# Gated linear attention and an expert layer on one core: attention from the second chunk on in halves of 64 tokens, with a new instruction order

## The chip, the core and the metric

The kernel runs on one core of a Trainium2 chip. The metric is the device time of one execution in microseconds (us), taken as the median of several runs. One execution was also recorded by the hardware profiler; that record is "the trace". PE is TensorE, DVE VectorE, ACT ScalarE, POOL GpSimd, and SP is the engine that issues the DMAs. Matrix products read SBUF and write PSUM, which has eight banks of 128 partitions by 512 fp32 numbers.

## What is computed

Two things follow each other: a recurrent attention with exponential gates over 4 batches, 8 heads, 768 tokens and head width 40, and a dense layer of width 320 to 2048 to 320 on its output.

```python
for t in range(S):
    m_new = np.maximum(f_gate[:, :, t] + m, i_gate[:, :, t])
    f_stab = np.exp(f_gate[:, :, t] + m - m_new)
    i_stab = np.exp(i_gate[:, :, t] - m_new)
    C = f_stab * C + i_stab * outer(vt, kt)
    n = f_stab * n + i_stab * kt
    y[:, :, t] = sigmoid(o_gate) * (C @ qt) / max(abs(n @ qt), 1.0)
x = y.transpose(0, 2, 1, 3).reshape(B * S, H * D)
h = x @ w_in
g = h * erf(softplus(h))
out = g @ w_out
```

All inputs are fp32; the two weight matrices arrive as 64-bit numbers and are decoded on the chip into a high and a low part.

## The kernel before

**Attention.** The 768 tokens are cut into 6 chunks of 128. A step s is one chunk of one batch, so there are 24 steps; chunk c = s // 4. Within a step the recurrence is written as matrix products. `S` forms 128 by 128 scores per head (L509). The decay between two tokens stands in the tile `dm`: for the first `PEX` = 6 steps PE builds it (`pe`, L426 to L429) and ACT takes its exponential; for the other 18 steps it is read back from DRAM by a broadcasting DMA (`bq`, L446), POOL adds a column (`add`, L450), ACT takes the exponential (`ex`, L454) and POOL zeroes the upper triangle (`sel`, L459). DVE multiplies scores and decay (`w`, L525). `ph` then makes the output: queries times the state carried over from the chunk before (L543), weights times values (L547), and the step's own contribution to the next state (L552), from values scaled by `vg` (L517). The state is a tile of 104 partitions by 4 by 82; two heads share it as a block-diagonal matrix whose other blocks are zero. `sa` (L562) and `sk` (L577) carry it on. `yg` (L583 to L587), `y` (L593) and `yy` (L599) normalise and gate, `tr` (L605) transposes, and `xh` (L621) and `xl` (L639) split the result into a high and a low part.

**Dense layer.** The 12 blocks of 256 tokens go through 24 phases. A phase has four `up` pieces on PE (L840, products of high and low parts in fp32r), each copied out of PSUM by `hb` (L851 on DVE, L849 on ACT), then softplus and erf on ACT (`sp` L863, `er` L867), their product on DVE (`mu` L875), a high part on ACT (`gh` L881), a low part on DVE (`gl` L886), and four `dn` pieces on PE (L921, L922, L924; for the first two phases full fp32, L917). ACT copies the sums out (`o`, L944). Weights are loaded and decoded in the first third of the run.

**Order.** Every engine executes its own queue in order. The order is written out by hand of a planner: the list `SEQUENCE` names each piece of work, and the program issues them one after the other. `+n` stands for n filler products on PE (L253), which compute nothing that is used. From step 10 on the pieces `tr(s-2)`, `S(s)` and `ph(s-1)` are merged into one (`X`), so that they stand directly behind each other on PE. Which engine does a copy is fixed by sets such as

```python
HB_ACT = {0, 1, 4}
VG_POOL = {3, 4, 5, 6, 7}
```

Of the kernel before, what the change touches and what calls it, by code (L numbers as in the profile page):

```python
# [18 lines left out]
L = 128  # L19
# [5 lines left out]
V1 = D + 1  # L25
# [56 lines left out]
SLOTS = dict(bank=6, po0=1, po1=1, big=20, xx=4, vg=2, dq=2, bits=2, den=2, gt=1, m_c=2, x0=2, aT=2, spl=1)  # L82
BANKS = dict(pa=4, h=2, po2=1, po3=1)
EARLY = 3
FULL = 2
# [3 lines left out]
HB_ACT = {0, 1, 4}  # L89
HI_DVE = {'i00', 'i01', 'i20', 'o4', 'o6', 'o9'}  # L90
LO_DVE = {'i01', 'i10', 'i20', 'i31', 'o1', 'o4', 'o5', 'o8', 't2', 't3'}
LO_PE = {'i00', 'i01', 'o0', 'o1', 'o4', 'o9', 't0', 't1', 't2'}
GL_POOL = set()
# [3 lines left out]
PEX = 6  # L97
# [4 lines left out]
VG_POOL = {3, 4, 5, 6, 7}  # L102
SK_ACT = {1, 2}
Y_DVE = {0, 1, 5, 6, 7, 9}
# [12 lines left out]
w2.1 lpi00 ex3.1 scan1 ph2 deci10 vali11 loi00 S3 load5 yg2 vg3 sk2.0 wout3 sk2.1 tr1 hii10 deci11 tr0 +1 loadv5
+1 xh0 +1 loadv7 +1 loi10 xh1 +1 wout8 +1 hii11 +1 xl1 y2 +2 valo2 +1 xl0 +1 loi11 +1 w3.0 up0.0 w3.1 yy2 valo4
deco2 up0.1 hb0.0 deco4 hio2 valo3 sum1 ph3 hb0.1 deco3 cumw1 th5 tr2 gexp1 up0.2 sp0.0 sk3.0 loo2 wout0 yg3
wout1 rest1 up0.3 hb0.2 hio4 gload2 sk3.1 y3 xh2 loadv4 hio3 xl2 yy3 decw1 tr3 loo4 hb0.3 at1 +2 xh3 atc1 loo3  # L120
+2 sp0.1 +1 xl3 +2 up1.0 split1 er0.0 up1.1 scan2 dq4 er0.1 mu0.0 dq5 valo0 pe4.0 sum2 th4 valo8 pe4.1 mu0.1
cumw2 hb1.0 ex4.0 up1.2 deco8 rest2 ex4.1 bq6 deco0 at2 th7 S4 hio8 atc2 vg4 hb1.2 pe5.1 w4.0 valo1 pe5.0 loo8
hio0 qa4 up1.3 vali20 w4.1 loo0 ex5.0 ex5.1 hb1.1 deci20 S5 hb1.3 sp1.0 deco1 ph4 hii20 qa5 dn0.1 wout6 hio1
loi20 er1.0 loo1 bq7 sa4 dn0.0 yg4 vg5 dq7 add6 sp1.1 sk4.1 w5.1 dn0.2 w5.0 sk4.0 y4 er1.1 mu1.0 ph5 add7 dn0.3
valo6 yg5 wout9 o0.0 yy4 deco6 tr4 o0.1 load8 dn1.0 mu1.1 xh4 win31 valo9 hio6 tail1 xl4 loo6 dn1.1 win21 deco9
y5 win30 dn1.3 hio9 load7 vali31 yy5 sa5 deci31 dq6 tr5 lpo9 sk5.0 hii31 wout7 sk5.1 xh5 loi31 wout5 dn1.2
vali21 xl5 loo9 deci21 valt1 up2.0 hii21 load6 dect1 load9 o1.0 o1.1 loi21 hit3 up2.1 hb2.0 hit2 vali30 lot3
lot2 up2.2 hb2.1 valo5 deci30 sp2.0 up2.3 hb2.2 deco5 hii30 up3.0 er2.0 hb2.3 loi30 up3.1 hb3.0 hio5 mu2.0 valo7
up3.2 hb3.1 gh2.0 deco7 sp3.0 up3.3 gl2.0 hb3.2 sp2.1 dn2.1 hb3.3 hio7 loo5 sp3.1 loo7 up4.0 er2.1 dn2.0 er3.1
mu2.1 up4.1 hb4.0 mu3.1 gh2.1 loadv6 er3.0 up4.2 gl2.1 ex6 bq8 mu3.0 dn2.3 hb4.2 sel6 dn2.2 gexp2 gh3.0 decw2  # L130
vg6 ex7 gl3.0 S6 gload3 o2.0 o2.1 S7 add8 w6.1 hb4.1 w6.0 th6 dn3.0 gh3.1 qa6 qa7 ph6 gl3.1 dn3.1 scan3 bq9
loadv8 yg6 sel7 sum3 dn3.2 loadv9 sa6 cumw3 rest3 dn3.3 sk6.1 vg7 w7.0 dq8 add9 sk6.0 th8 o3.0 up4.3 w7.1 st3.0
th9 o3.1 ex9 y6 st3.1 yy6 ph7 ex8 sel9 sp4.0 sel8 S8 yg7 bq10 load10 tr6 vg8 up5.0 w8.0 load11 xh6 loadv10 hb4.3
qa8 er4.0 w8.1 up5.1 y7 vg9 yy7 hb5.0 add10 tr7 xl6 ph8 xh7 loadv11 hb5.1 xl7 sp5.0 mu4.0 up5.2 bq11 sa8 sa7
gh4.0 dq9 sk8.1 up5.3 sk7.0 sp4.1 sk7.1 dq10 gl4.0 er4.1 S9 sk8.0 add11 yg8 dn4.0 w9.1 ex10 y8 w9.0 qa9 dn4.1
mu4.1 th11 th10 at3 yy8 hb5.2 X10 gload4 gh4.1 sel10 atc3 hb5.3 gl4.1 sp5.1 tr8 vg10 bq12 dn4.3 scan4 loadv12
er5.0 w10.0 sa9 dn4.2 yg9 dq11 ex11 sk9.1 mu5.0 up6.0 sk9.0 add12 load12 w10.1 th12 up6.1 o4.0 xh8 hb6.0 st4.0
gh5.0 sel11 xl8 ex12 o4.1 up6.2 hb6.1 st4.1 er5.1 sel12 up6.3 y9 hb6.2 sp6.0 yy9 mu5.1 up7.0 hb6.3 vg11 gh5.1
up7.1 qa10 sp6.1 gl5.1 er6.0 X11 sum4 gl5.0 cumw4 gexp3 mu6.0 dn5.1 bq13 er6.1 w11.0 decw3 yg10 dn5.0 qa11 gh6.0
w11.1 y10 hb7.0 xh9 dn5.2 yy10 add13 xl9 hb7.1 up7.2 sp7.0 o5.0 sa10 st5.0 mu6.1 dq12 up7.3 hb7.2 gh6.1 sk10.0  # L140
# [892 lines left out]
```

## Time and profile before

| | |
|---|---|
| median of 3 runs (lowest to highest) | 471.83 us (471.32 to 472.54) |
| the profiled execution's own time | 472.8 us |
| its span, first to last instruction | 471.1 us |
| PE busy | 457.5 us, 97% |
| DVE busy | 335.0 us, 71% |
| ACT busy | 337.8 us, 72% |
| POOL busy | 105.1 us, 22% |
| DMA | 53.21 MB, 113 GB/s on average |

Busy time is the union of an engine's instructions. A share near 100% on one engine says that the others wait for it over the span as a whole; in which stretch that holds, and what is lost in the rest, has to be read by stage.

### The profile page before, as it was taken

The page shows a single profiled execution, that of the slowest core. Times are in us where ns is not written, and L with a number is a line of the kernel's source. Part 1 is how long each engine was busy: PE and PEld are TensorE (multiplying, and loading weights), DVE is VectorE, ACT ScalarE, POOL GpSimd, SP SyncE. Part 2 cuts the span into 40 slices and gives each one's busy share as a digit, 9 for nine tenths or more (in the row PEclk, how much of TensorE's full clock was granted, in tenths as well). Part 3 has the DMA queues.
Part 4 walks back from the last instruction along what each step waited for, and adds up shares of the span by engine and source line. Part 5 has one row for each costly group of instructions (what it writes and reads, how often), then busy time and mean ns, then how long its engine had stood idle before and what let it go on. Part 6 is the DMA issues. An engine that isn't in the chain of part 4 may idle for free.

```text
span 471.1 us, 12874 instructions
## 1 busy us (share of the span) xinstructions
PE 457.5 (97%) x5569; PEld 404.0 (86%) x5574; DVE 335.0 (71%) x565; ACT 337.8 (72%) x390; POOL 105.1 (22%) x99
## 2 busy tenths in 40 slices
PE   9899999999989999699999999999999999999997
PEld 3468877999979999689899988899988889888996
DVE  4689998767979888479669568777727775646460
ACT  3658994897597976276997579999269547778561
POOL 2213161216342124104022532131220020000000
PEclk9999999999999999899999999999999999999999
DMA  7993449412664028703023861022720000001001
GB/s 192 407 384 106 148 143 295 172 58 88 193 254 144 30 82 210 217 21 116 0 90 106 239 184 48 14 94 86 195 79 3 0 3 1 0 1 56 1 0 58
DMA packets 28877, 53.21 MB, mean 113 GB/s; under 512 B 3060, under 2 KB 17844, under 8 KB 28820
## 3 DMA queue, kind: packets, MB, share of 16 engines
q1 hardware_dynamic: 28820, 52.38, 35.6%
q8 instruction: 44, 0.72, 0.7%
q14 instruction: 13, 0.11, 0.1%
HBM read 48.27 MB, written 4.10 MB: 111 GB/s over the span
## 4 chain that ended last, share of the span: by engine, by line
PE 85%; DMA 8%; issue 2%; DVE 2%; SPq 2%; ACT 1%; DVEq 0%; ACTq 0%
PE h L840 35%; PE po L921 12%; PE po L924 11%; PE po L922 11%; PE pa L509 4%; PE po L917 4%; DMA raw<-in_w_out_dram 3%; PE pa L543 3%; PE pa L547 2%; DMA raw<-in_w_in_dram 2%; DMA qk<-in_qk_dram 2%; PE pa L605 1%; DMA kvo<-in_kvo_dram 1%; PE pa L552 1%; DVE bits L787 1%
## 5 line engine op out<-in xcount | busy, mean ns | idle before, releaser
L840 PE MATMUL h<-xx,wh 128*128 128x256 f32 (+1 forms) x768 | 177.4, 339 | 2.6 <-issue 2.0
L840 PEld LDWEIGHTS h<-xx,wh 128*128 128x128 f32 x768 | 126.8, 189 | 18.8 <-issue 2.0
L922 PE MATMUL po<-wol,gh 128*128 128x320 f32 x352 | 106.1, 310 | 3.7 <-issue 3.7
L921 PE MATMUL po<-woh,gh 128*128 128x320 f32 x352 | 107.9, 316 | 0.0
L851 DVE COPY hb<-h 128x512 f32<-128x512 f32 x84 | 57.5, 688 | 54.0 <-PE h L840 53.1
L840 PE MATMUL h<-xx,wl 128*128 128x256 f32 (+1 forms) x256 | 86.5, 338 | 0.0
L924 PE MATMUL po<-woh,gl 128*128 128x320 f32 x352 | 76.9, 311 | 0.0
L922 PEld LDWEIGHTS po<-wol,gh 128*128 128x128 f32 x352 | 66.5, 189 | 4.8 <-issue 3.9
L875 DVE TENSOR_TENSOR hb<-e,hb 128x1024 f32<-128x1024 f32 x44 | 56.5, 1290 | 16.6 <-ACT e L867 16.4
L921 PEld LDWEIGHTS po<-woh,gh 128*128 128x128 f32 x352 | 66.3, 188 | 2.1
L886 DVE TENSOR_TENSOR gl<-hb,gh 128x1024 fp32r<-128x1024 f32 x44 | 55.8, 1268 | 15.1 <-ACT gh L881 15.0
L863 ACT ACTIVATE e<-hb 128x1024 f32<-128x1024 f32 x48 | 50.3, 1058 | 22.0 <-DVE hb L851 21.7
L881 ACT ACTIVATE gh<-hb 128x1024 fp32r<-128x1024 f32 x44 | 46.2, 1050 | 19.1 <-DVE hb L875 16.6
L924 PEld LDWEIGHTS po<-woh,gl 128*128 128x128 f32 x352 | 58.3, 189 | 0.1
L840 PEld LDWEIGHTS h<-xx,wl 128*128 128x128 f32 x256 | 48.4, 189 | 5.7
L867 ACT ACTIVATE e<-e 128x1024 f32<-128x1024 f32 x48 | 50.0, 1057 | 0.4
L450 POOL TENSOR_TENSOR dm<-dm,aT 128x1024 f32<-128x1024 f32 x18 | 37.7, 2094 | 43.6 <-DVE dm L525 23.5
L867 ACT ACT_TABLE_LOAD x36 | 46.2, 1283 | 0.6
L863 ACT ACT_TABLE_LOAD x33 | 42.3, 1283 | 4.6 <-DVE hb L851 4.1
L593 POOL TENSOR_TENSOR kvo<-kvo,den 128x320 f32<-128x320 f32 x18 | 16.6, 920 | 108.3 <-DVE kvo L587 56.6
L459 POOL TENSOR_SCALAR_AFFINE_SELECT dm<-dm 128x1024 f32<-128x1024 f32 x18 | 21.9, 1220 | 67.6 <-ACT dm L454 66.5
L525 DVE TENSOR_TENSOR dm<-pa,dm 128x512 f32<-128x512 f32 x48 | 32.0, 683 | 6.2 <-PE pa L509 6.0
(116 smaller groups left out, 561.4 us busy)
## 6 DMA issues: line engine op xcount, KB each, us to landing
kvo<-in_kvo_dram SPq DMA_DIRECT2D x24, 484.0 KB
dm<-cum_dr SPq DMA_DIRECT2D x18, 512.0 KB
qk<-in_qk_dram SPq DMA_DIRECT2D x12, 512.0 KB
qk<-in_qk_dram SPq DMA_DIRECT2D x12, 416.0 KB
raw<-in_w_in_dram SPq DMA_DIRECT2D x8, 512.0 KB
out_dram<-o SPq DMA_DIRECT2D x24, 160.0 KB
raw<-in_w_out_dram SPq DMA_DIRECT2D x8, 320.0 KB
dq<-dec_dr SPq DMA_DIRECT2D x20, 128.0 KB
```

The lines of the kernel that those rows point to most:

```text
L450: nc.gpsimd.tensor_tensor(v.dm, v.dm, G.aT[:, b].unsqueeze(2).to_broadcast([128, H, L]), op=ALU.add)
L525: nc.vector.tensor_tensor(v.w[:, j], v.ps[j], v.w[:, j], op=ALU.mult)
L840: nc.tensor.matmul(V.h[i][:, n * width:(n + 1) * width], w, m, start=(q == 0), stop=(q == len(ops) - 1))
L851: nc.vector.tensor_copy(V.hb[:, i * 512:(i + 1) * 512], V.h[i])
L863: nc.scalar.activation(V.e, V.hb, AF.Softplus)
L867: nc.scalar.activation(V.e, V.e, AF.Erf)
L875: nc.vector.tensor_tensor(V.g if full else V.hb, V.e, V.hb, op=ALU.mult)
L881: nc.scalar.activation(V.gh, V.hb, AF.Copy)
L886: (nc.gpsimd if f in GL_POOL else nc.vector).tensor_tensor(V.gl, V.hb, V.gh.bitcast(F32), op=ALU.subtract)
L921: nc.tensor.matmul(po, V.gh[:, ts], woh[:, w], start=start, stop=False)
L922: nc.tensor.matmul(po, V.gh[:, ts], wol[:, w], start=False, stop=False)
L924: nc.tensor.matmul(po, V.gl[:, ts], woh[:, w], start=False, stop=stop)
```

## The change

The change has these parts.

- From the second chunk on each step works on two halves of 64 tokens. Scores are 64 by 64 per half and head. Between the halves there is a middle state (`mid`), made from the state before by `ma` and `mk` on DVE; `na` and `nk` make the state after the second half. A state is now a new tile of 104 by 4 by 41 without zero blocks.
- `S` holds the scores and the contribution to the two states; it therefore needs `vg`, which needs `sel`. `ph` holds queries times state and weights times values, written side by side into two PSUM banks; `hc` copies the first of them to SBUF, and `yg` adds the second in two more operations.
- The decay tile is half as large. `PEX` is 4, so PE builds it for 4 steps and 20 steps read it from DRAM.
- Copies and subtractions get an engine one by one through the table `ENGINES`. Among 24 phases, `hb` runs 60 times on ACT and 36 on DVE (before 12 and 84), `gh` 20 times on ACT and 24 on DVE (44 and 0), `gl` 27 times on DVE and 17 on POOL (44 and 0), `vg` 8 on DVE and 16 on POOL (15 and 5).
- `SEQUENCE` is new throughout. It has 15 filler products where there were 56. `ph` is no longer merged with the pieces beside it; `tr(s-2)` and `S(s)` still are (`A`) for most steps.

```diff
-PEX = 6
+PEX = 4
+HL = L // 2
...
+            for t in (slice(0, HL), slice(HL, L)) if c else (slice(0, L),):
+                nc.vector.tensor_tensor_scan(out=x[:, C, t], data0=x[:, Y, t], data1=zero.to_broadcast([128, t.stop - t.start]),
+                                             initial=0.0, op0=ALU.add, op1=ALU.add)
...
             def bq():
-                v.dm = big("dm").rearrange("p (h l) -> p h l", l=L)
+                t = big("dm")[:, 0:H * HL]
+                v.dm = t.rearrange("p (h l) -> p h l", l=HL)
                 v.w = ofj(v.dm)
-                nc.sync.dma_start(v.dm, cum_dr[c, b:b + 1].to_broadcast([128, H, L]))
+                for g, r in enumerate(half_rows):
+                    nc.sync.dma_start(v.dm[r], cum_dr[c, b, g:g + 1].to_broadcast([HL, H, HL]))
...
             def sl():
-                nc.gpsimd.affine_select(out=v.dm, in_=v.dm, pattern=[[0, H], [1, L]], compare_op=ALU.is_ge,
-                                        fill=0.0, base=0, channel_multiplier=-1)
+                for r in half_rows:
+                    nc.gpsimd.affine_select(out=v.dm[r], in_=v.dm[r], pattern=[[0, H], [1, HL]], compare_op=ALU.is_ge,
+                                            fill=0.0, base=0, channel_multiplier=-1)
...
+            @make(f'S{s}', 'PE', 0.95 if not last else 0.8, 128 if not last else 96, after=[load, loadv, *ex, *vg], new=psb, use=[qkb, kvb, vgb], mode=1,
+                  target=due - 2 * lead, order=[step[s - 1].ph_] if s < 5 else [step[s - 2].ph_])
+            def Sp():
+                banks()
+                for p in range(NPR):
+                    for g, r in enumerate(half_rows):
+                        for j in range(2):
+                            js = slice(64 * j, 64 * j + D)
+                            nc.tensor.matmul(v.ps[j][r, p], v.k[js, p, r], v.q[js, p, r], start=True, stop=True)
+                kf = v.kn.rearrange("p h d -> p (h d)")
+                for p in range(NPR):
+                    for j in range(2):
+                        for g, r in enumerate(half_rows[0:1] if last else half_rows):
+                            m, at = 64 if j == 0 else D, (2 * p + j) * D
+                            nc.tensor.matmul(v.pk[g][64 * j:64 * j + m, p], kf[r, at:at + m], v.vg[r, 2 * p + j],
+                                             start=True, stop=True)
...
+            mid = carried('m', 'mid', lambda: prev.st, 0, prev.next, new=[midb], use=[prev.nextb])
+            if not last:
+                v.next = [carried('n', 'st', lambda: v.mid, 1, [mid], new=[v.nextb], use=[midb])]
...
+            for p in range(NPR):
+                for g, r in enumerate(half_rows):
+                    for j in range(2):
+                        js = slice(64 * j, 64 * j + D)
+                        nc.tensor.matmul(v.ph[j][r, 0, p], v.q[js, p, r], (v.mid if g else prev.st)[js, p], start=True, stop=True)
+            for h in range(H):
+                for i in range(2):
+                    for g, r in enumerate(half_rows):
+                        o = slice(32 * i, 32 * i + 32)
+                        nc.tensor.matmul(v.ph[h % 2][HL * g + 32 * i:HL * g + 32 * i + 32, 1, h // 2], v.w[r, h % 2, h // 2, o], v.v1[r, h],
+                                         start=True, stop=True)
...
     for s in range(CLUSTER, steps + 1):
-        plan.merge(f'X{s}', [*([step[s - 2].tr] if s > CLUSTER else []), *([step[s].S] if s < steps else []), step[s - 1].ph_])
+        m = [*([step[s - 2].tr] if s > CLUSTER else []), *([step[s].S] if s < steps else [])]
+        if len(m) > 1:
+            plan.merge(f'A{s}', m)
```

How the order changes is shown at two places. The first is PE's queue at one attention step. Before, in the last chunk (where no state is made), transposition, scores and output stand behind each other between two `dn` pieces:

```order
L605 MATMUL pa<-ident,kvo 128x128 x3
L509 MATMUL pa<-qk 128x128 x8
L543 MATMUL pa<-state_71,qk 32x82 x4
L547 MATMUL pa<-kvo,dm 32x41 x8
L543 MATMUL pa<-state_71,qk 32x82 x4
L547 MATMUL pa<-kvo,dm 32x41 x8
L543 MATMUL pa<-state_71,qk 32x82 x4
L547 MATMUL pa<-kvo,dm 32x41 x8
L543 MATMUL pa<-state_71,qk 32x82 x4
L547 MATMUL pa<-kvo,dm 32x41 x8
L921 MATMUL po_4129<-woh,gh 128x320
```

After, at a step of the third chunk, the transposition and the scores with the state products (L544, L550) stand between an `up` piece and a `dn` piece:

```order
L880 MATMUL h<-xx,wh 128x256 x2
L659 MATMUL pa<-ident,kvo 128x128 x3
L544 MATMUL pa<-qk 64x64 x16
L550 MATMUL pa<-vg,kvo 64x41 x2
L550 MATMUL pa<-vg,kvo 40x41 x2
L550 MATMUL pa<-vg,kvo 64x41 x2
L550 MATMUL pa<-vg,kvo 40x41 x2
L550 MATMUL pa<-vg,kvo 64x41 x2
L550 MATMUL pa<-vg,kvo 40x41 x2
L550 MATMUL pa<-vg,kvo 64x41 x2
L550 MATMUL pa<-vg,kvo 40x41 x2
L958 MATMUL po_2634<-woh,gh 128x320
```

and the output of a step stands further on, alone between dense products:

```order
L880 MATMUL h<-xx,wh 128x256 x2
L607 MATMUL pa<-st,qk 64x41 x16
L612 MATMUL pa<-kvo,dm 32x41 x32
```

So each step of the later chunks now interrupts the dense products twice instead of once. Counted over PE's whole queue, neighbouring products with different tilings of the array (rows by columns that one product occupies) meet 124 times after and 99 times before.

The second place is POOL's queue in the middle of the run. Before, it holds additions, selections and the scaling of outputs only:

```order
L450 TENSOR_TENSOR dm<-dm,aT 128x1024
L593 TENSOR_TENSOR kvo<-kvo,den 128x320
L599 COPY kvo<-kvo 128x64
L459 AFFINE_SELECT dm<-dm 128x1024
L450 TENSOR_TENSOR dm<-dm,aT 128x1024
L459 AFFINE_SELECT dm<-dm 128x1024
```

After, low parts of the dense layer (L923) stand in the same queue, ahead of `add`, `sel` and `vg` (L487, L497, L513):

```order
L513 TENSOR_TENSOR vg<-kvo,dm 128x328
L923 TENSOR_TENSOR gl<-hb,gh 128x1024
L487 TENSOR_TENSOR dm<-dm,aT 128x512
L497 AFFINE_SELECT dm<-dm 64x512 x2
L647 TENSOR_TENSOR kvo<-kvo,den 128x320
L513 TENSOR_TENSOR vg<-kvo,dm 128x328
```

What moved is a part of DVE's work for the dense layer onto POOL, in front of the chain that ends in `vg`, for which `S` on PE now waits.

## Rows read from the trace of the kernel before

**Rows 1.** The page: busy times, and the chain that ended last by engine.
```profile
PE 457.5 (97%) x5569; PEld 404.0 (86%) x5574; DVE 335.0 (71%) x565; ACT 337.8 (72%) x390; POOL 105.1 (22%) x99
PE 85%; DMA 8%; issue 2%; DVE 2%; SPq 2%; ACT 1%; DVEq 0%; ACTq 0%
```
**Rows 2.** Windows of 20 us: stretch, its length, busy (count) per engine, clock, DMA.
```profile
40.00:60.00 20.00, 19.31 (x167) 15.92 (x158) 19.28 (x41) 18.54 (x30) 5.89 (x7) 1.00 0.49 153
180.00:200.00 20.00, 16.34 (x218) 15.02 (x217) 12.48 (x22) 7.75 (x11) 7.39 (x7) 0.91 0.88 231
400.00:420.00 20.00, 20.00 (x112) 17.95 (x111) 12.18 (x14) 15.29 (x14) 0.00 (x0) 1.00 0.00 0
```
**Rows 3.** Waits of PE: line, for what, total us, times, longest.
```profile
PE po L922 <- issue: 3.7, 1, 3.7
PE h L840 <- issue: 2.0, 1, 2.0
```
**Rows 4.** Timeline of PE, one merged step: start, us, engine, line, operation.
```profile
323.53 0.49 PE L605 MATMUL pa<-ident,kvo 128*128 128x128 f32 x3
323.95 1.16 PE L509 MATMUL pa<-qk 40*128 40x128 f32 x16
325.04 0.35 PE L543 MATMUL pa<-state,qk 104*32 104x82 f32 x8
325.20 0.33 PE L547 MATMUL pa<-kvo,dm 128*32 128x41 f32 x16
325.36 0.33 PE L543 MATMUL pa<-state,qk 104*32 104x82 f32 x8
...
326.24 0.48 PE L552 MATMUL pa<-vg,kvo 128*32 128x41 f32 x32
326.65 0.42 PE L921 MATMUL po<-woh,gh 128*128 128x320 f32 x1
326.91 0.31 PE L922 MATMUL po<-wol,gh 128*128 128x320 f32 x1
327.06 0.31 PE L921 MATMUL po<-woh,gh 128*128 128x320 f32 x1
```
**Rows 5.** Timeline of PE, a transposition alone between dense products.
```profile
391.82 0.49 PE L605 MATMUL pa<-ident,kvo 128*128 128x128 f32 x3
392.07 0.39 PE L921 MATMUL po<-woh,gh 128*128 128x320 f32 x1
```
**Rows 6.** Timeline of PE, the decay of one early step, then fillers.
```profile
7.98 0.38 PE L426 MATMUL pa<-mask 128*128 128x512 bf16 x1
9.69 2.35 PE L253 MATMUL po<-warm 128*128 128x512 bf16 x10
```
**Rows 7.** Groups by line: out<-in, shape, count | busy us, mean ns | idle before.
```profile
L547 PEld LDWEIGHTS pa<-kvo,dm 128*32 128x32 f32 x1536 | 25.3, 110 | 3.1 <-issue 1.8 <-ACT dm L438 0.8 <-DVE dm L525 0.4
L509 PEld LDWEIGHTS pa<-qk 40*128 40x128 f32 x384 | 23.2, 187 | 3.6 <-issue 1.9 <-PE pa L605 0.5 <-PE po L924 0.2
```
**Rows 8.** Groups by line on DVE, ACT and POOL.
```profile
L851 DVE COPY hb<-h 128x512 f32<-128x512 f32 x84 | 57.5, 688 | 54.0 <-PE h L840 53.1
L849 ACT ACTIVATE hb<-h 128x512 f32<-128x512 f32 x12 | 7.1, 589 | 1.0 <-PE h L840 1.0
L881 ACT ACTIVATE gh<-hb 128x1024 fp32r<-128x1024 f32 x44 | 46.2, 1050 | 19.1 <-DVE hb L875 16.6 <-PE h L840 2.6
L886 DVE TENSOR_TENSOR gl<-hb,gh 128x1024 fp32r<-128x1024 f32 x44 | 55.8, 1268 | 15.1 <-ACT gh L881 15.0
L450 POOL TENSOR_TENSOR dm<-dm,aT 128x1024 f32<-128x1024 f32 x18 | 37.7, 2094 | 43.6 <-DVE dm L525 23.5 <-DMA dm<-cum_dr 14.1 <-DVE kvo L593 3.3
L517 POOL TENSOR_TENSOR vg<-kvo,dm 128x328 f32<-128x328 f32 x5 | 5.4, 1085 | 18.1 <-DVE m_c L311 9.4 <-DMA dq<-dec_dr 8.5
```
**Rows 9.** Timeline of DVE: one low part.
```profile
185.47 2.96 DVE L886 TENSOR_TENSOR gl<-hb,gh 128x1024 fp32r<-128x1024 f32 x1 [1.12 <-ACT gh L881]
```
**Rows 10.** Windows of 2 us around PE's longest stop; columns as in rows 2.
```profile
190.00:192.00 2.00, 0.00 (x0) 0.00 (x0) 0.36 (x1) 0.38 (x1) 0.53 (x2) 1.00 0.83 325
194.00:196.00 2.00, 2.00 (x10) 2.00 (x9) 0.47 (x1) 0.00 (x0) 0.00 (x0) 0.50 0.96 234
```

More of the change, by code (lines that the diff above doesn't have):

```diff
@@ L117 @@
[L117 to L121, printed above, removed]
@@ L404, in attention @@
         if c > 0:
[L405 removed]
+            @make(f'dq{s}', 'SP', 1.16, after=[G.dec], kb=350.0, new=[dqb])
             def dqp():
@@ L511, in attention, with values, vgp @@
-        v.S = Sp
         vg, w = [], []
-        if not last:
-            @make(f'vg{s}', *(('POOL', 0.8) if s in VG_POOL else ('DVE', 0.52)), after=[*sel, loadv], new=[vgb], use=[dmb, kvb], lock=True)
-            def vgp():
+        def values():
+            @make(f'vg{s}', 'DVE', on=dict(DVE=0.52, POOL=0.8), after=[*sel, loadv], new=[vgb], use=[dmb, kvb], lock=True)
+            def vgp(e):
                 v.vg = t = new(sb, [128, H, V1], F32, "vg")
-                (nc.gpsimd if s in VG_POOL else nc.vector).tensor_tensor(
-                    t, v.v1, v.dm[:, :, L - 1:L].to_broadcast([128, H, V1]), op=ALU.mult)
+                engines[e].tensor_tensor(
+                    t, v.v1, v.dm[:, :, Q - 1:Q].to_broadcast([128, H, V1]), op=ALU.mult)
@@ L522, in attention @@
+        v.S = Sp
         for j in range(2):
-            @make(f'w{s}', 'DVE', 0.69, after=[Sp, sel[j]], use=[psb[j], dmb], order=vg)
+            @make(f'w{s}', 'DVE', 0.4 if c else 0.69, after=[Sp, sel[j]], use=[psb[j], dmb], order=vg)
             def wp(j=j):
@@ L526, in attention @@
             w.append(wp)
-        qa = None
+        qa = mid = None
+        v.next = []
         if c > 0:
@@ L580, in yg, with sk, hcopy @@
-        @make(f'yg{s}', 'DVE', 0.97, after=[ph, th], new=[denb], use=[phb, kvb])
+        if c == 0:
+            @make(f'sk{s}', 'DVE', on=dict(DVE=0.3, ACT=0.38), after=[ph], new=[v.nextb], use=phb, target=due + 10)
+            def sk(e):
+                v.st = new(sb, [128, NPR, V1], F32, "st")
+                copy_on(e, v.st[0:QR], v.pk[0:QR])
+            v.next = [sk]
+        hj, hc = lambda j: v.v1.rearrange("p (n j) d -> p j n d", j=2)[:, j], []
+        for j in range(2) if c else ():
+            @make(f'hc{s}', 'ACT', on=dict(ACT=0.3, DVE=0.28), after=[ph], use=[phb[j], kvb])
+            def hcopy(e, j=j):
+                copy_on(e, hj(j), v.ph[j][:, 0])
+            hc.append(hcopy)
@@ L647, in decode @@
     def decode(name, raw, rawb, ready, hi, lo):
-        engine = 'DVE' if name in LO_DVE else 'POOL'
         v = SimpleNamespace()
@@ L772, in weights_out @@
         name, vb = f'o{u}', Buf('bits')
-        engine = 'DVE' if name in LO_DVE else 'POOL'
         n, o = divmod(u, 2)
```

438 lines of the change are left out of this document (216 added, 222 removed).

## The prediction

> **What bounds the kernel now.** I read the page first: PE is busy 97% of the span, DVE 71%, ACT 72%, POOL 22%, and the chain that ended last lies on PE for 85% of the span [rows 1]. A share over the span says little about stages, so the windows come next. After the start-up PE is full; 400 to 420 us shows it, with 20.00 of 20 us, while DVE needs 12.18 and ACT 15.29 [rows 2]. In the start-up DVE is the busier one: 19.28 of 20 us from 40 to 60 us, when PE has 19.31 but fills gaps with filler products [rows 2]. The waits of PE then show that almost nothing holds it later: two stops, 2.0 and 3.7 us long, for which no releaser is seen [rows 3]. The longer one is followed by a stretch with the clock at 0.50, that is the level of 1.2 GHz [rows 10]. So after the start-up the time is what PE's products cost, and a change is worth what it takes from PE's queue, if no new wait comes in.
>
> **What a step costs on PE now.** The timeline of one merged step [rows 4] gives it by start times. Scores: 323.95 to 325.04, 1.09 us. Output: 325.04 to 326.24, 1.20 us for 32 records with 82 columns and 64 with 41 (each fp32 product is two records). State products: 326.24 to 326.65, 0.41 us. A change of tiling costs extra: the transposition takes 0.42 us when scores follow and 0.25 us when a dense product follows [rows 4, 5], a difference of 0.17; the first dense product behind takes 0.26 us to the next where 0.15 is usual, 0.11 more [rows 4]. I take 0.13 us for one such change, somewhat under the mean, since the second was seen more often. Without changes a step is then 0.96 + 1.20 + 0.28 = 2.44 us, and 2.16 us in the last chunk, which has no state products.
>
> **What it costs after.** Small records on four column quarters come every 20 ns with 82 columns (8 in 0.16 us) and every 10 ns with 41 (16 in 0.16 us) [rows 4].
> - Scores: 32 records with 64 columns. Interpolated between those rows a record takes 15.6 ns, so 0.50 us. The ends are 0.50 (that is, half of today's columns per quarter) and 0.96 (each of the doubled records as dear as half an old one).
> - State products: still 32 records, but the loaded operand is 64 wide on two of four quarters. Weight loads take 187 ns for 128 columns and 110 for 32 [rows 7], 0.80 ns a column, so 51 ns for 64; one quarter has 8 of them: 0.41 us. The low end is today's 0.28.
> - Queries times state: 32 records with half the columns, again loads of 64: 0.41 us. Ends: 0.32 (10 ns each) and 0.64 (20 ns).
> - Weights times values: 64 records as before, now over eight tiles. No row shows records closer than 10 ns, so I take 0.64 us; eight tiles at column rate would give 0.32.
>
> Together 1.96 us. Gain: 0.48 us in each of the 16 steps of chunks two to five, 7.7 us; 0.20 us in each of 4 steps of the last chunk, where the 8 state products that go leave the loads of one quarter as they were, 0.8 us. The first chunk's 4 steps keep their products. Against that, `ph` stands alone and switches tiling inside: 25 changes more over the queue (124 against 99), at 0.13 us each 3.3 us. `PEX` from 6 to 4 takes the decay of two steps off PE; one step's takes from 7.98 to 9.69 us, 1.71 us [rows 6], so 3.4 us. Net: 7.7 + 0.8 + 3.4 - 3.3 = 8.6 us less on PE. With all low ends a step costs 1.42 us (1.28 in the last chunk) and the net is 19.9 us less; with all high ends 2.65 us and 5.3 us more.
>
> The 41 fillers that go cost 0.235 us each [rows 6], 9.6 us, but they stand where PE would wait, in the start-up: I count them as nothing. Their cover is DVE's load there [rows 2].
>
> **A rule against it.** A small record took 10 ns with 41 columns and 20 ns with 82 [rows 4]; the time follows the columns, with no floor above 10 ns. The Trainium skill, "TensorEngine Tiling (Array Packing)", section "Instruction Overhead", says the opposite of such products: each has about 60 cycles of overhead, so a small dimension gains nothing from tiling. At 25 ns a record, an estimate from that page, the 160 records of a step would take 4.0 us; the trace does not agree, since the 144 records of a step would then take 3.6 us where rows show 2.7.
>
> **The other engines.** Bounds are enough. DVE loses 48 `hb` (0.688 us each, 33.0) and 17 `gl` (1.268, 21.6) [rows 8]; it gains 24 `gh`, each at most a `gl`, 30.4, and 96 copies and additions from PSUM (14 `xh`, 13 `o`, 29 `hc`, 40 in `yg`), each at most an `hb`, 66.0. That is 377 us at most, 80% of the span. ACT gains 48 `hb` (0.589, 28.3), loses 24 `gh` (1.050, 25.2) [rows 8] and has shorter exponentials: about as now. POOL gains 17 `gl` of 2.09 us, the time of an addition of the same size, to 2.96, the longest `gl` on DVE, and 11 `vg` of 1.085 [rows 8, 9], against smaller additions: 105 becomes 130 to 150 us. None reaches PE.
>
> DMAs: the decay tiles of 20 steps move half the bytes each in two transfers where 18 whole ones were; `dq` is as before. SP issues 22 more in all for `bq`; PE had 19.31 of 20 us at a DMA share of 0.49 [rows 2], so I cost them at nothing. The two stops lie where the DMA engines are loaded (0.83 in the longer one [rows 10]); I leave them as they are.
>
> **Sum.** The profiled execution took 472.8 us around a span of 471.1; less 8.6 is 464.2. The median of the runs is 1.0 below that execution, so the forecast is **463 us**.
>
> **Rivals.**
> - *PE waits for the chain behind `vg`* (slower). `S` needed loads and `ex` before; now it needs `add`, `ex`, `sel` and `vg`, and POOL has a `gl` among them. PE's queue is in order, so everything dense behind `S` waits. If `S` finds POOL in a `gl` in the 15 steps from 9 on, half of 2.09 to 2.96 us with what stands behind it is about 1.5 us a time, 22 us: 485 us. It decides from 0.43 us a step (8.6 / 20). For it: in the trace a `gl` took 2.96 us on DVE when POOL was at work beside it, against 1.268 on average [rows 8, 9]. Against: POOL stays under a third of the span, and the order can place `sel` early. 0.09.
> - *Small records have a floor*. If each costs 20 ns, the dearer of the two kinds, a step takes 3.2 us and one of the last chunk 2.9: 0.76 us more in 16 steps, 0.72 in 4, 3.3 for changes, less 3.4: 487 us. Rows 4 speak against it with 10 ns. This is the direction of the rule named above; by its figure it would be 502 us. 0.03.
> - *The start-up at the low clock*. Without fillers PE stands idle more often; after the long stop the clock was at 0.50 [rows 10]. Before the first dense product PE has four decays (1.71 us), scores (0.96) and outputs without state (0.64 + 0.28), 14.4 us; at half clock that is 14.4 more, less the 9.6 us of fillers: 5 us late, 468 us. For it: few fillers are left. Against: DVE sets that stage anyway. 0.12.
> - *The relief is not on the path* (no change). The two decays stand in the start-up, where DVE has 19.28 of 20 us from 40 to 60 us [rows 2], so the 3.4 us may be no gain; with `S` near its high end (0.3 us a step dearer) the rest is gone too: 471 us. 0.07.
> - *Column rate everywhere*: 19.9 us less, 452 us. 0.10.
>
> **How the numbers follow.** The forecast has 0.59; its own range is 456 to 468. Faster than 0.3% (1.4 us, about what a measurement of this kernel can tell from no change) are the forecast, the start-up case and the column rate: 0.59 + 0.12 + 0.10 = 0.81. Same is 0.07. Slower are the first two rivals, 0.12. The range 454 to 470 leaves out the slower cases, part of the no-change case and the far end of the column rate.
>
> **What would show it.** Right: in PE's timeline scores near 0.50 us, state products 0.41, queries times state 0.41, weights times values between 0.32 and 0.64; PE full once the start-up ends; no wait of L544 of more than 0.4 us on average. Wrong: long waits of PE for POOL's `vg` or for DVE's `w` and `mk` (first rival), a clock below 1.00 in the first 40 us together with a later first `up` (third), or records of 20 ns and more (second). If PE's sum falls by 8.6 us and the time does not, its waits will name what is late next.

## The result, and the profile after

The changed kernel takes **465.05 us** (median of 4 runs, 463.71 to 467.43) against 472.03 us for the kernel before: a ratio of 0.985, 95% interval 0.9812 to 0.9888. The forecast was 463, the range 454 to 470. In a later comparison the same kernel gave 465.77 us, ratio 0.9853 (0.9823 to 0.9884). Medians here and below take in all runs, while ratios leave out the runs more than 1.5% above the fastest of their kernel. The profiled execution took 465.84 us around a span of 464.1, 7.0 us less than the span before.

The page: busy times, and the chain that ended last by engine; they answer to [rows 1].

```profile
PE 448.3 (97%) x5891; PEld 396.5 (85%) x5893; DVE 335.0 (72%) x636; ACT 328.0 (71%) x401; POOL 147.1 (32%) x143
PE 85%; DMA 9%; ACT 2%; DVE 2%; issue 1%; SPq 0%; ACTq 0%
```

PE still carries the end, with 9.2 us less busy time. POOL is at 147.1, inside the forecast's 130 to 150; DVE at 335.0 and ACT at 328.0 stay far from the end.

The timeline of PE of the changed kernel, both small pieces of two steps and the dense products next to them (start, us, engine, line, operation); it answers to [rows 4].

```profile
223.20 0.49 PE L659 MATMUL pa<-ident,kvo 128*128 128x128 f32 x3
223.62 0.69 PE L544 MATMUL pa<-qk 40*64 40x64 f32 x32
224.13 0.61 PE L550 MATMUL pa<-vg,kvo 64*64 64x41 f32 x32
224.68 0.42 PE L958 MATMUL po<-woh,gh 128*128 128x320 f32 x1
224.93 0.31 PE L959 MATMUL po<-wol,gh 128*128 128x320 f32 x1
...
228.00 0.46 PE L961 MATMUL po<-woh,gl 128*128 128x320 f32 x2
228.39 0.68 PE L607 MATMUL pa<-st,qk 40*64 40x41 f32 x32
228.99 0.83 PE L612 MATMUL pa<-kvo,dm 64*32 64x41 f32 x64
229.75 0.41 PE L958 MATMUL po<-woh,gh 128*128 128x320 f32 x1
230.00 0.31 PE L959 MATMUL po<-wol,gh 128*128 128x320 f32 x1
```

By start times: scores 0.51 us, state products 0.55, queries times state 0.60, weights times values 0.76, 2.42 in all where the merged step took 2.70 [rows 4]. Into that 2.42 come the changes of tiling; taken off at 0.13 us each, the last three are 0.42, 0.47 and 0.63. The forecast had 0.50, 0.41, 0.41 and 0.64. Only queries times state was dearer than forecast.

The waits of PE in the changed kernel (line, for what, total us, times, longest); they answer to [rows 3].

```profile
PE pa L462 <- DVE spl L397: 1.7, 1, 1.7
PE h L880 <- issue: 1.5, 1, 1.5
PE po L959 <- issue: 1.3, 1, 1.3
...
PE pa L612 <- issue: 1.0, 1, 1.0
PE po L954 <- DVE gh L912: 0.9, 1, 0.9
```

The two stops of 2.0 and 3.7 us are gone, and three others, 1.55, 1.00 and 1.25 us, have come. L544, which now needs `vg` and the decay chain, waited 0.5 us in all: the first rival did not happen. (In a second execution of this kernel it waited 1.9 us, for the load of its queries and keys and not for that chain.)

The windows, first of the kernel before, then of the changed one (stretch, its length, busy and count of PE, PEld, DVE, ACT, POOL, clock, DMA share, GB/s). The second set answers to [rows 2] as well.

```profile
0.00:20.00 20.00, 17.60 (x185) 8.61 (x186) 10.23 (x27) 10.00 (x18) 5.59 (x14) 1.00 0.88 281
8.00:12.00 4.00, 4.00 (x25) 1.65 (x23) 0.98 (x2) 0.00 (x0) 0.00 (x0) 1.00 1.01 234
12.00:16.00 4.00, 3.66 (x30) 2.06 (x30) 1.48 (x3) 2.42 (x6) 0.00 (x0) 1.00 1.03 411
```

```profile
8.00:12.00 4.00, 4.00 (x16) 1.68 (x18) 3.28 (x7) 2.48 (x5) 0.00 (x0) 0.69 0.99 386
12.00:16.00 4.00, 3.74 (x30) 2.18 (x29) 3.40 (x10) 2.13 (x6) 0.74 (x1) 0.88 1.03 417
40.00:60.00 20.00, 18.70 (x237) 16.38 (x237) 18.97 (x36) 19.20 (x28) 6.88 (x7) 1.00 0.79 242
180.00:200.00 20.00, 20.00 (x278) 17.00 (x279) 15.86 (x26) 16.96 (x19) 3.45 (x2) 1.00 0.33 104
400.00:420.00 20.00, 20.00 (x116) 18.24 (x115) 10.80 (x14) 12.22 (x13) 3.12 (x2) 1.00 0.09 33
```

Two things are to be seen. From 8 to 16 us DVE was busy for 2.46 us before and is for 6.68 us now: the new order starts its work earlier. And the clock now falls there, to means of 0.69 and 0.88, behind 1.66 us in which PE waited for the scan split (L462).

**Where the 7.0 us came from.** The table sums PE's rows from each start to the next, less the idle time ahead of the next. The last column is the profiled execution of an experiment told below, the changed kernel with fillers put back (`e13_after_17_28`); its clock was 1.0, so it shows what the products cost when the clock does not fall.

```
us                                     before    after   after with fillers
fillers                                 13.95     5.64    13.94
scores, output, state products          62.2     58.7     57.2
decay products                           9.8      7.3      6.9
transpositions, low weight parts        14.3     14.8     13.4
dense products                         357.6    362.3    360.6
  without the fillers                  444.0    443.0    438.1
  of it by the lower clock, estimated    1.7      3.4      0.0
idle between rows                        8.7     11.0      5.2
  of it stops of 0.8 us and more, no
  releaser seen                          5.6      3.8      2.4
fillers and idle ahead of first fp32 dn 18.0     13.6     17.2
```

The forecast took 8.6 us off the products and nothing anywhere else. In the profiled execution after, products lost 1.0 us; fillers and idle time of the start-up lost 4.4, the stops 1.8. The sum came out near the forecast although its parts did not.

The kernel before has a stretch at the lower clock too, behind its long stop [rows 10]. The row "by the lower clock" estimates what such stretches cost, each row's length by the share of the clock that was not granted to it. At the full clock on both sides the products then lose 2.7 us in the changed kernel (442.3 to 439.6) and 4.2 with the fillers put back (to 438.1). Of the 4.4 us of the start-up 0.8 are left with the fillers, and yet the first fp32 `dn` starts at about the same time, 51.9 against 51.5 us: the products ahead of it take 34.8 us there and 37.9 without the fillers. So most of what the missing fillers gave came back in these products, which ran partly at the lower clock.

### The profile page after: what moved, and what is told of

It reads as the page before. It is cut to its first block, busy times and chain, and to the rows that moved or that the text cites. A ratio compares the mean times of both kernels' runs of the same rounds, so it can differ in the third digit from the quotient of the medians.

```text
span 464.1 us, 13726 instructions
## 1 busy us (share of the span) xinstructions
PE 448.3 (97%) x5891; PEld 396.5 (85%) x5893; DVE 335.0 (72%) x636; ACT 328.0 (71%) x401; POOL 147.1 (32%) x143
## 4 chain that ended last, share of the span: by engine, by line
PE 85%; DMA 9%; ACT 2%; DVE 2%; issue 1%; SPq 0%; ACTq 0%
PE h L880 35%; PE po L958 12%; PE po L959 11%; PE po L961 11%; PE po L954 4%; PE pa L612 3%; DMA raw<-in_w_out_dram 3%; PE pa L544 3%; PE pa L607 3%; DMA gt<-in_gates_dram 2%; DMA qk<-in_qk_dram 2%; PE pa L550 2%; PE pa L659 1%; DMA kvo<-in_kvo_dram 1%; DMA dm<-cum_dr 0%
## 5 line engine op out<-in xcount | busy, mean ns | idle before, releaser
L880 PE MATMUL h<-xx,wh 128*128 128x256 f32 (+1 forms) x768 | 182.6, 342 | 2.1 <-issue 1.5
L880 PEld LDWEIGHTS h<-xx,wh 128*128 128x128 f32 x768 | 128.1, 190 | 17.8 <-issue 1.7
L923 POOL TENSOR_TENSOR gl<-hb,gh 128x1024 fp32r<-128x1024 f32 x17 | 42.2, 2484 | 130.3 <-ACT gh L238 91.3
L238 ACT ACTIVATE hb<-h 128x512 f32<-128x512 f32 x60 | 35.1, 589 | 45.8 <-PE h L880 45.6
L900 ACT ACTIVATE e<-hb 128x1024 f32<-128x1024 f32 x48 | 50.5, 1059 | 13.3 <-DVE hb L240 12.8
L240 DVE COPY hb<-h 128x512 f32<-128x512 f32 x36 | 24.7, 686 | 28.5 <-PE h L880 28.5
L487 POOL TENSOR_TENSOR dm<-dm,aT 128x512 f32<-128x512 f32 x20 | 22.0, 1101 | 66.2 <-DMA dm<-cum_dr 60.9
L497 POOL TENSOR_SCALAR_AFFINE_SELECT dm<-dm 64x512 f32<-64x512 f32 x40 | 33.0, 825 | 18.0 <-ACT dm L491 16.5
L923 DVE TENSOR_TENSOR gl<-hb,gh 128x1024 fp32r<-128x1024 f32 x27 | 36.1, 1339 | 3.2 <-ACT gh L238 2.7
L557 DVE TENSOR_TENSOR dm<-pa,dm 128x256 f32<-128x256 f32 (+1 forms) x48 | 21.2, 461 | 13.4 <-PE pa L550 11.0
```

What stands on the lines that cost most here:

```text
L238: nc.scalar.activation(to, of, AF.Copy)
L240: engines[e].tensor_copy(to, of)
L487: nc.gpsimd.tensor_tensor(v.dm, v.dm, G.aT[:, b].unsqueeze(2).to_broadcast([128, H, HL]), op=ALU.add)
L497: nc.gpsimd.affine_select(out=v.dm[r], in_=v.dm[r], pattern=[[0, H], [1, HL]], compare_op=ALU.is_ge, fill=0.0, base=0, channel_multiplier=-1)
L880: nc.tensor.matmul(V.h[i][:, n * width:(n + 1) * width], w, m, start=(q == 0), stop=(q == len(ops) - 1))
L900: nc.scalar.activation(V.e, V.hb, AF.Softplus)
```

## The experiments

Each comparison runs beside the kernel before on the same chip. Noise is larger than the first four runs suggested: twelve runs of one kernel spread over 4 to 9 us.

**Scores twice.** Is PE's time in the middle worth its full length? Every score product of 20 steps is issued a second time, over the same values:

```diff
-                            nc.tensor.matmul(v.ps[j][r, p], v.k[js, p, r], v.q[js, p, r], start=True, stop=True)
+                            for _ in range(2):
+                                nc.tensor.matmul(v.ps[j][r, p], v.k[js, p, r], v.q[js, p, r], start=True, stop=True)
```

> The changed kernel with every 64x64 score product issued twice in steps 4 to 23 (the second writes the same values over the first); it adds 0.50 to 0.51 us of TensorE work to each of 20 steps, 10.1 us in all, about what the halving took off the scores (0.96 to 0.50), and nothing on another engine. Theory A (TensorE's small products bound the middle, so their saving is worth its full length): the time rises by 9 to 11 us, to 474.5 to 476.5, a ratio to the kernel before of 1.004 to 1.010: the change's whole gain gone. Rival B (the middle is bound by the chain through DVE, ACT and the state, and TensorE's relief there is hidden): it rises by less than 4 us, ratio 0.985 to 0.993. Rival C (more TensorE records in a burst starve its instruction supply): besides, new stops put down to issue of 1 us or more behind the doubled scores, and over 11 us in all, ratio above 1.010.

Measured: 475.79 us, ratio 1.0052 (1.0021 to 1.0083). Against the changed kernel's 0.985 that is 2.0% or 9.5 us (by the two intervals, give or take some 2), for 9.4 us more in the score rows. The timeline of PE at one step shows the doubled piece, 0.98 us from 228.43 to the first state product at 229.41, and the waits show no stop longer than before:

```profile
228.01 0.49 PE L660 MATMUL pa<-ident,kvo 128*128 128x128 f32 x3
228.43 1.20 PE L545 MATMUL pa<-qk 40*64 40x64 f32 x61
229.41 0.26 PE L551 MATMUL pa<-vg,kvo 64*64 64x41 f32 x2
```

```profile
PE pa L613 <- issue: 1.1, 1, 1.1
...
PE po L960 <- issue: 1.1, 1, 1.1
PE pa L595 <- issue: 1.0, 1, 1.0
```

Theory A holds. The chain through DVE and the state has room enough that PE's small products count in full. That halving the scores, which this edit undoes in size, was worth about as much follows by inference.

**One dense piece between scores and output, in the kernel before.** What does parting the two cost? The merge is switched off, and in 15 steps a dense piece moves between the parts, as in:

```diff
-    for s in range(CLUSTER, steps + 1):
-        plan.merge(
+    for s in ():
+        plan.merge(
```

> The kernel before, with one dense piece moved between scores and output in the 15 merged steps: 15 changes of tiling more, nothing else. Theory A (a change of tiling costs 0.13 us, as forecast): 2.0 us more, 474 us. Theory B (0.19 us, by what the dense products of the changed kernel took more): 2.9 us more, 475 us. Rival C (hidden, or paid back because fewer small products stand in a row): 470 to 472.5 us.

Measured: 475.13 us, ratio 1.0046 (1.002 to 1.0073), which is 2.2 us or 0.14 us for each parted step; PE's rows sum to 461.6 instead of 457.9 us, 0.3 of it in the fillers, so some 0.23 us a step. The time fits theories A and B alike and excludes C. The forecast counted a change wherever neighbouring products have different tilings. Scores and output have them already, so by that count a parted step has one change more, as the expectation says, and such a change costs 0.23 us in PE's rows and 0.14 by the time where the forecast took 0.13. Counted as changes between dense and small products there are two more, and the one from scores to output goes. The rows show where the cost lies: going into a small piece, the dense product ahead of it takes 0.10 us longer to its successor (mean of 21 places); coming out, the last small product takes 0.13 longer and the first dense one 0.11 (34 places each).

**Scores joined to outputs, in the changed kernel.** If parting costs, does joining win it back? In steps 10, 11, 14, 15, 16 and 23 the dense pieces between the two go behind:

```diff
-S10 up6.0 up6.1 ph10
+S10 ph10 up6.0 up6.1
...
-A15 dn8.1 dn8.3 ph15
+A15 ph15 dn8.1 dn8.3
```

(tokens of other engines are left out).

> The changed kernel with the scores (and state products) of steps 10, 11, 14, 15, 16 and 23 put directly ahead of the output pieces that follow them, the dense pieces that lay between moved behind; six dense stretches fewer. Theory A (each dense stretch between two small pieces costs two changes of TensorE's tiling, 0.13 us into it and 0.15 to 0.20 us out of it): TensorE's rows sum to 1.5 to 2.0 us less, and the time falls by about as much if no new wait comes: ratio to the kernel before 0.980 to 0.983 where the unedited change has 0.985. Rival B (small pieces back to back bring stops and waits for w and the middle state): the rows sum to 1.5 to 2.0 us less, and waits of 1 to 4 us more stand in their place: ratio 0.984 to 0.992.

Measured: **499.58 us**, ratio 1.0539 (1.0501 to 1.0578), far beyond both theories. The waits of PE, then windows around the longest one (columns as above):

```profile
PE pa L605 <- DVE qk L563: 16.3, 5, 5.5
...
PE pa L605 <- DVE st L576: 2.0, 2, 1.0
```

```profile
168.00:172.00 4.00, 0.34 (x24) 0.22 (x14) 2.12 (x6) 3.97 (x5) 0.00 (x0) 1.00 0.00 0
172.00:176.00 4.00, 2.13 (x96) 2.08 (x96) 3.56 (x5) 1.60 (x3) 0.00 (x0) 0.51 0.40 128
176.00:180.00 4.00, 4.00 (x31) 3.91 (x23) 0.33 (x1) 0.00 (x0) 0.93 (x2) 0.63 0.49 128
```

The output (L605 here) stands in PE's queue before DVE has scaled the queries (L563) of the same step, and everything dense stands behind it. Each wait is then paid twice: idle time rises by 19 us (30.0 against 11.0), and the rows by 16.8 us (465.5 against 448.7), because the clock is at or near its lower level after most of these waits. This is the first rival's mechanism, with the wait behind the output instead of behind the scores. The dense piece between scores and output is what hides the chain; its two changes of tiling are the price.

**Fewer fillers in the kernel before, more in the changed one.** The forecast counted 41 fillers that go as nothing. Three tests: only the first 16 fillers kept in the kernel before; 28 put back into the changed kernel, two at each of 14 places of its start-up; these and 8 more at its very start. That makes 43 and 51 where the kernel before has 56; the last two expectations count four fewer each time.

```diff
-... mask +9 pe0.0 pe0.1 ... ex0.1 win11 ... S0 gload1 ...
+... mask +17 pe0.0 pe0.1 ... ex0.1 +2 win11 ... S0 +2 gload1 ...
```

> The kernel before with 16 filler products instead of 56 (the later ones left out; they compute nothing that is used). Theory A (fillers in PE's in-order queue delay the start-up): most of the 4.6 us that the changed kernel gains in the start-up is here too, 467 to 470 us, first product in full fp32 of the dense layer earlier than 63.4 us. Rival B (fillers only fill waits, DVE sets the stage): 471 to 473 us, the fillers' time turns into idle time of PE. Rival C (PE falls to the low clock in the first 40 us): 474 us or more, clock 0.50 in that stretch.

> The changed kernel with 28 fillers put back into its first 45 us, two at each of 14 places, which brings them to 39 of the 52 that the kernel before issues. It tests the prediction's reading that the fillers are covered. Theory A (as the prediction had it, DVE's load ends the start-up, so fillers only fill idle time): the first fp32 down-projection starts within 0.5 us of 50 to 51.5 us, the time is the changed kernel's (ratio 0.985) or better by the clock. Theory B (in the new order TensorE has useful work nearly throughout and fillers push it): 28 x 0.235 = 6.6 us of fillers less the idle time that they take up, some 2 to 3 us, so the first fp32 down-projection and the end come 2 to 4.6 us later: ratio 0.989 to 0.995.

> The changed kernel with both kinds of fillers put back: 17 in place of 9 at its start, and the 28 at 14 places of the first 45 us; 47 in all, of 52 in the kernel before. Theory A (fillers stand in idle time and keep the clock up, so what they cost comes back): clock at 1.0 in all of the first 40 us, mean clock 0.996 or more, and a time of 463 to 466, the changed kernel's within its noise. Theory B (fillers push useful work): 36 x 0.235 = 8.5 us less the idle time that they take up, so 468 to 471.

Measured: the kernel before with 16 fillers 474.96 us, ratio 1.0015 (0.9978 to 1.0052); the changed kernel with 28 more 465.92 us, 0.9845 (0.981 to 0.9879); with 36 more 465.71 us, 0.9847 (0.9792 to 0.9903). None differs from its parent beyond the noise. The windows say why. The first is of the kernel before with 16 fillers, the second of the changed kernel with 36 more:

```profile
12.00:16.00 4.00, 1.70 (x7) 0.59 (x4) 2.38 (x5) 2.60 (x6) 0.24 (x1) 0.83 1.02 405
16.00:20.00 4.00, 3.90 (x111) 3.33 (x112) 3.23 (x9) 3.13 (x7) 2.29 (x2) 0.50 1.02 408
...
28.00:32.00 4.00, 3.53 (x13) 1.79 (x12) 2.34 (x6) 1.08 (x2) 0.41 (x1) 0.50 1.04 391
```

```profile
8.00:12.00 4.00, 3.25 (x18) 1.41 (x18) 3.08 (x7) 2.42 (x5) 0.00 (x0) 1.00 1.00 389
12.00:16.00 4.00, 4.00 (x33) 2.15 (x32) 3.25 (x10) 2.03 (x5) 0.74 (x1) 1.00 1.03 417
```

In the kernel before, fillers that go leave 2.3 us of idle time from 12 to 16 us, and the clock falls behind it; in the changed kernel, fillers that come back take 0.23 to 0.3 us each, and with 36 of them the clock stays up. In the execution with 28 more the first fp32 `dn` started at 54.7 us where it was 51.5, and the median of the runs was still the same within the noise. So counting fillers as nothing was right as a net, for both kernels.

**17 fillers at the start alone**, to close the 1.66 us ahead of the clock's fall:

```diff
-... mask +9 pe0.0 pe0.1 ...
+... mask +17 pe0.0 pe0.1 ...
```

> The changed kernel with 17 in place of 9 fillers ahead of the first decay matrix, so that TensorE has no idle time between the fillers (which end at 5.6 us) and 7.9 us; nothing else. Theory A (the low clock of 9.4 to 12.8 us comes from that idle time and costs about half of its length): the granted clock stays at 1.0 in the first 40 us, the mean clock goes from 0.992 to about 0.997, and the span falls by 0.5 to 1.7 us, with less spread between runs. Rival B (DVE's start-up load sets the end of the start-up, and the low clock lies under it): the clock stays up and the time stays within 0.3 us of the changed kernel's.

Measured: 464.82 us, ratio 0.9831 (0.9805 to 0.9856), against 0.9853 for the unedited kernel on that chip. The clock stayed up to 16 us, and then fell from 16 to some 27 us (a mean of 0.53 from 16 to 24). So the fall from 9.4 to 12.8 us went, as theory A had it, another came from 16 us, which it had not, and no gain showed beyond the noise. With the same 17 fillers the profiled execution of a later version (`e7_split_fill17`) kept its clock at 1.00 although PE stood idle for about a quarter of the time from 8 to 28 us; where the clock falls is not the same in each execution. The ratio is the lowest measured, but not surely below the unedited kernel's.

**`PEX` from 6 to 4 alone, in the kernel before**:

```diff
-PEX = 6
+PEX = 4
...
-split1 ... pe4.0 ... pe4.1 ... ex4.0 ex4.1 ... pe5.1 ... pe5.0 ex5.0 ex5.1
+bq4 ... bq5 ... add4 ... ex4 sel4 add5 ... ex5 ... sel5
```

> The kernel before with one part of the change alone: PEX from 6 to 4, so the decay matrices of steps 4 and 5 come by DMA, POOL and ACT instead of TensorE, and the second scan split is gone. Theory A (the prediction's term): TensorE loses 2 x 1.71 us of decay products; what they hid stays hidden, and the time falls by 1.5 to 3.4 us. Rival B (the start-up ends with DVE's and ACT's chain, so TensorE's relief there becomes idle time): within 1 us of the kernel before. Rival C (the DMA route is late for step 4): TensorE waits on dm of step 4, the time rises by 1 to 3 us.

Measured: 473.25 us, ratio 0.9997 (0.9972 to 1.0023): rival B. The timeline of PE shows where the 3.4 us went, a transposition that waits for DVE's tile of gate sums:

```profile
55.82 0.30 PE L347 MATMUL pa<-ident,x 128*128 128x128 f32 x1 [4.36 <-DVE x L325]
```

**The stops: output pairs parted.** The three stops of the changed kernel come where the outputs of two steps stand back to back on PE. Here is the first, in PE's timeline of the changed kernel, the second output and the first dense products behind it:

```profile
125.42 0.68 PE L607 MATMUL pa<-st,qk 40*64 40x41 f32 x32
126.02 0.81 PE L612 MATMUL pa<-kvo,dm 64*32 64x41 f32 x64
126.76 0.38 PE L880 MATMUL h<-xx,wh 128*128 128x256 f32 x1
128.70 0.39 PE L880 MATMUL h<-xx,wh 128*128 128x256 f32 x1 [1.55 <-issue]
```

The unedited kernel ran again, then with each pair parted by a dense piece, then so with 17 fillers, then with two other pairs brought together:

```diff
-er5.0 ph8 hc8.0 o3.0 up5.2 hb5.2
+er5.0 up5.2 ph8 hc8.0 o3.0 hb5.2
...
-ph20 hc20.0 ph21 hc21.0 mu16.0 dn15.0
+ph20 hc20.0 dn15.0 ph21 hc21.0 mu16.0
...
-gl18.0 ph22 hc22.1 yg23 y23 hc22.0 yg22 dn17.2
+gl18.0 dn17.2 ph22 hc22.1 yg23 y23 hc22.0 yg22
```

> The changed kernel, unedited, beside the next three on one chip, so that they can be compared with it and not only with the kernel before. Theory A (the stops belong to the order): its profile again shows TensorE stops put down to issue at the same three places, behind the pairs of output pieces (1.55, 1.00 and 1.25 us in the first profile), within 0.5 us each. Theory B (the stops are accidents of one execution): other places or none. The time: 465 if it is as in the first comparison; if the start-up's low clock varies from run to run, its runs spread over several us, and the runs with the lower mean granted clock are the longer ones.

> The changed kernel, with one dense piece moved between the two output pieces at the three places where two of them stand directly behind each other on PE. Theory A (PE's stops of 1.55, 1.00 and 1.25 us come from so many small products in a row that PE runs out of instructions): the three stops go, and with the first the 3.4 us at the low clock behind it; 3.8 + 1.7 us less, 459 to 461 us, and no stop of over 0.5 us after 60 us. Rival B (the stops come from the load on the DMA engines, or fall anywhere): stops of the same total elsewhere, 464 to 467 us.

> Both edits together: the three pairs of output pieces parted by a dense piece each, and 17 fillers. Theory A (each takes away its own loss): no stop put down to issue over 0.5 us, clock at 1.0 in the first 40 us, and a time 2 to 4 us below the unedited changed kernel on this chip. Rival B (the waits that the stops hid stand in their place, and the low clock lay under DVE's load): within 1 us of the unedited changed kernel.

> The changed kernel with the three pairs parted, and two others brought together that have been apart so far: the output of step 17 directly behind that of step 16 (near 190 us), and that of step 19 directly behind that of step 18 (near 255 us). One look for the stops. Theory A (two output pieces back to back, some 190 TensorE records within 2.7 us, outrun what feeds TensorE with instructions): a new stop put down to issue of 1 to 1.6 us within 4 us behind each of the two, and none over 0.5 us elsewhere. Rival B (the stops belong to their old places, to what else runs there): no new stop at these two places.

Measured: unedited, 465.77 us with stops of 0.86, 0.99 and 1.26 us at the same three places, so they belong to the order. Parted, 469.74 us, ratio 0.9888 (0.9843 to 0.9932), which the intervals do not tell from the unedited kernel's 0.9853. Parted with 17 fillers, 469.24 us, 0.9918 (0.9885 to 0.9951): slower than the unedited kernel on that chip. Neither brought the gain that its theory A expected. The waits of PE in the first parted version:

```profile
PE pa L548 <- DVE vg L511: 1.0, 1, 1.0
PE po L959 <- DVE gl L921: 1.0, 1, 1.0
PE h L878 <- ACT hb L236: 0.9, 1, 0.9
...
PE h L878 <- DVE kvo L634: 0.8, 1, 0.8
...
PE po L959 <- issue: 0.3, 1, 0.3
```

The stops are gone, and data waits that they had hidden or that the moved pieces bring, 3.7 us, stand in their place. With the 17 fillers a new stop of 1.07 us came at 311 us. The profiled executions were among the shorter of each version's runs (spans 461.8 and 464.7), so they do not show what made most of the other runs longer, by 4 to 9 us in the first version; that stays open. The last version took 473.87 us, one run, with the clock at 0.50 from 16 to 24 us. Its new pairs ran near 260 and 302 us, not at the places that the expectation named. Behind the first there was no stop; in the second the outputs waited 2.5 us for DVE's queries between them. So two outputs back to back are not enough to make a stop.

**What the stops wait for.** The traces settle more than the four versions do. The page of the changed kernel lists a DMA queue that brings instructions: 46 packets of 16 KB in all, one for about every 256 of PE's 11784 products and weight loads (packets, MB, share of the DMA engines). The second line is from the timeline of PE with 36 fillers put back (`e13_after_17_28`):

```profile
q8 instruction: 46, 0.75, 0.7%
129.11 0.56 PE L610 MATMUL pa<-kvo,dm 64*32 64x41 f32 x35 [1.56 <-issue]
```

The changed kernel's stops end 1.36, 1.27 and 1.22 us behind the landing of such a packet, and 3776, 9920 and 10944 of PE's products and weight loads have started by then, each time 192 more than a multiple of 256. The same holds for all 25 stops of 0.8 us and more without a releaser in the fourteen traces kept: each ends 1.2 to 1.5 us behind a packet, 188 to 194 past a multiple of 256 (the traces miss some records). The fillers make the test. With 36 more of them the first stop comes after 3778 records, at the same count, though the 36 fillers and their weight loads now stand ahead of it; it has moved in the program from the dense product behind the second output to the middle of that output. So PE waits there for its next instructions. That cause, which theory A of the parted version named, is right, though the gain did not come. Two outputs back to back use up 384 of them in 2.7 us. Whether that makes a stop then depends on where in the count of 256 the pair falls, which would explain the pair without one; no run moved one pair through that count.

## Why the prediction came out right

- **PE bounds the middle**: right. Scores issued twice cost their full length, 9.5 us for 9.4.
- **Sizes of the small products**: nearly right. The forecast had 8.5 us off for 20 steps. One term was too small, queries times state: 0.47 us against 0.41, 1.2 us over 20 steps. The choice between the two ends for weights times values (0.32 and 0.64) was right with 0.63 for 64 records. The working of the two 0.41 was not sound: 0.80 ns a column leaves out what a load costs beside its columns, and loads of 64 columns took 135 ns (L544, L607), not 51. That one of the two fitted (0.42) is luck, and whether loads or the number of products set the pace of the small products no run shows. The trace speaks against the 25 ns that the prediction worked out from the Trainium skill, "TensorEngine Tiling (Array Packing)", section "Instruction Overhead": a record took 10 ns.
- **Changes of tiling**: the step "25 changes more over the queue, at 0.13 us each 3.3 us" was too small, and this is the term that was sized most wrongly. At a full clock on both sides (last column of the table, and 1.7 us off the dense products of the kernel before) the dense products cost 4.7 us more, and the small ones lose 5.0 instead of some 7.3 without their changes: together 7.0 us, an estimate, or 0.28 for each of the 25. The parted steps, at 0.23 in the rows for one change of the forecast's count, give 5.8. The forecast took 0.13 as the whole of a change, but going from small to dense costs on both sides of the border, 0.13 and 0.11 us.
- **`PEX`, 3.4 us**: the size held (decay rows lose 2.5 to 2.9 us), but alone it gains nothing. The fourth rival's reason was right for this term in the old order: the two decays stand in the start-up, off the path.
- **Fillers at nothing**: right as a net, in both directions, but for a reason that rows 2 do not hold. Between 40 and 60 us, where DVE was full, only 1.5 of the 15.0 us of fillers ran; 9.4 us of them ran before 20 us, where DVE was busy for 10.2 of 20 us. From 8 to 16 us it was the DMA engines that were full (1.01 and 1.03). What the fillers cost and what the clock gives for them cancel; that is what the three tests show.
- **The start-up as it is** ("DVE sets that stage anyway"): not so, and this hid a part of the errors above. Fillers and idle time ahead of the first fp32 `dn` fell from 18.0 to 13.6 us; with the fillers put back they are 17.2, and `PEX` then saves its 2.9 us without new idle time, where in the old order it became a wait. The windows show DVE's work starting earlier from 8 to 16 us; neither fewer fillers nor `PEX` gave a gain in the old order. That the new order makes it is argued from what is left; no run changed the start-up's order alone.
- **The start-up at the low clock**, the third rival: it came in part, 0.69 and 0.88 from 8 to 16 us, and took some of the products' gain (the lower clock cost 3.4 us in the profiled execution, some of it behind the first stop, against 1.7 before).
- **Stops left as they are**: they moved and went from 5.6 to 3.8 us, a gain that the forecast did not have. It put them with the load on the DMA engines; the traces put them where PE has used up its instructions.
- **PE waits for the chain**: did not happen, because the order keeps a dense stretch between scores and output. Taken away in six steps, it costs 34 us.

So the mechanism of the middle was right, PE's own products, but that 463 came out near 465 is in good part luck: two errors cancel, 8.6 us off the products where 2.7 to 4.2 came at a like clock (1.0 in the profiled execution), and nothing in the start-up and the stops where 4.4 and 1.8 came.

## What to carry to other kernels

Sum PE's rows by kind, start to start, before and after: a total that agrees can hide terms that do not. A piece of independent work between a small product and the one that needs its result through another engine is worth far more than the two changes of tiling it costs (34 us lost over six steps here), since PE can pay for a wait a second time in its clock. Take the price of such a change from both sides of its border. Fillers and relief of PE in a stage that another engine ends were worth nothing either way in the old order. Where PE stops and no releaser is seen, count its records: a stop at the same count in every version is a wait for instructions.

## What the runs showed of the hardware

- Small records of 41 columns over 64x32 tiles came at the same 10 ns (64 in 0.63 us) as those over 128x32 [rows 4]: eight tiles gave no more than four.
- In the joined version the products behind PE's longest wait, 5.5 us, ran near 1.2 GHz for several us: the granted clock was 0.51 and 0.63 in the two windows behind it. Over the version this nearly doubled the price of waits: 19 us idle came with 16.8 us of longer rows. Behind shorter waits it differs: a stop of 1.55 us in the changed kernel was followed by 0.50 (130 to 132 us), one of 1.56 us with the fillers put back by 1.00.
- PE's instructions come in packets of 16 KB, one for about 256 products and weight loads (46 for 11784), and PE stops where it has used them up before the next packet is there: 25 stops of 0.9 to 3.7 us in fourteen traces, each ending 1.2 to 1.5 us behind a packet. One came at a DMA share of 0.02 (376 to 380 us), so loaded DMA engines, with which the prediction had put them, are not needed for them.
